# An FFT filter with two dense networks: the opening laid out anew, weight chunks in another order, and the projection's matmuls in runs

## The chip, the cores and the metric

The kernel runs on one core of one Trainium2 chip. The core's engines, with the names that the profile gives them, are TensorE (PE, its weight loads PEld), VectorE (DVE), ScalarE (ACT), GpSimd (POOL) and SyncE (SP), which issues the DMAs. The metric is the device time of one execution in microseconds (us); the time of a kernel is the median of its runs.

## The reference, cut to what matters

Eight batches of 3072 tokens with 256 features pass a filter in the frequency domain along the tokens, then a network with a softmax-weighted hidden layer and a norm, then a network with a gated hidden layer.

```python
X = np.fft.rfft(x, axis=1)                      # x: 8 x 3072 x 256
y = np.fft.irfft(X * (filt_r + 1j * filt_i)[None], n=3072, axis=1)
x = y.reshape(8 * 3072, 256)
h = x @ w_in                                    # 256 -> 1024
e = np.exp(h - h.max(-1, keepdims=True))
solu = h * (e / (e.sum(-1, keepdims=True) + 1e-09))
mu, var = solu.mean(-1, keepdims=True), solu.var(-1, keepdims=True)
x = ((solu - mu) / np.sqrt(var + 1e-06) * g_ln) @ w_out    # 1024 -> 256
h = x @ w_in2                                   # 256 -> 2048
out = (h * (1.0 / (1.0 + np.exp(-1.702 * h)))) @ w_out2    # 2048 -> 256
```

The four weight matrices come as 64-bit floats (the kernel sees words of 64 bits), all else as 32-bit floats.

## The kernel before, in words

**The filter.** A transform of 3072 points is done as 128 x 24. `Filter` takes one or two batches. `load_x` loads a piece of x (128 x 512), `step1` multiplies it by the first transform matrix `dft1`, and `store_a` writes the result to `a_d` in DRAM; a batch has twelve pieces. Then come 32 groups of 96 rows. For each, `load_gt` loads the group's row block (a forward and an inverse matrix of 96 x 96, and the filter's real and imaginary part, 256 columns each), `load_bt` loads its rows of `a_d`, `forward` multiplies by the forward matrix, the product is weighed with the filter, `inverse` multiplies by the inverse matrix, and `store_z` writes z to DRAM. Batch 0 goes alone, as `EarlyFilter`, in plain 32-bit matmuls (each is recorded as two); the others go in pairs, mostly with operands split into a high and a low part (`split`). In `EarlyFilter` POOL copies the halves of the forward matrix in swapped order (`split_m`), a second matmul with this copy (`swap`) gives the rows with real and imaginary part exchanged, and DVE forms the weighed product with three operations (in `forward`, `swap` and `weigh`).

**The weights.** `Weights` cuts the matrices into 24 chunks of 128 x 512 words (512 kB each): four of w1, four of w2, eight of w3, eight of w4, in this order. A chunk is loaded (`load`) into a staging tile (`STAGE`), turned from 64 to 32 bits by DVE operations on its two halves (`magnitude`, `sign`, `lower`, `add`), in w2 and w4 scaled on ACT (`scale_rows`), and split into a high part by ACT (`split_hi`) and a low part by DVE (`split_lo`).

**The networks.** `First(n)` handles block n of 256 tokens, 96 blocks in all: it loads its rows of z, applies the last inverse transform (`y`), multiplies by w1 (`hidden`), computes the softmax weighting and the norm, exchanges blocks through DRAM (`shuffle`, `gather`) and transposes (`turn`), splits (`u_hi`, `u_lo`), and multiplies by w2 (`project`), of which x2s is made. `Second` handles block 0 alone, then pairs of blocks, and the last one alone: 8 or 16 steps of `hidden` with w3, `tanh`, `gate`, two splits and `output` with w4, then `finish` and `store`.

**The order.** No scheduler chooses it. Every step is put into a list with a due time; the list is sorted by due time and the steps are issued in that order, so that on each engine and on SP's queue the program order is the order of due times. One block of `First` has 16 units of due time. The due times of the opening are in `EARLY`: `start1` and `start2` are where batch 0's pieces and groups begin, `end` is where they end, `loads` and `weights` place the chunks. All DMAs are issued by SP, which waits in order: where an issue has to wait for data, all behind it wait too.

```python
end, step1, step2 = v["end"], v["step1"], v["step2"]
start2 = end - v["gap"] - step2 * NG
start1 = start2 - step1 * N2 / 2
```

The projection multiplies, for each half c of its output and each eighth kk of the hidden layer, one w2 high part by 512 columns (high and low part of u) and one w2 low part by 256 columns (the high part of u), all added up in one PSUM tile; two calls per c take four kk each.

Of the kernel before, what the change touches and what calls it, by code (L numbers as in the profile page):

```python
# [83 lines left out]
STAGE = [i % 5 if i < 15 else i % 3 for i in range(24)]  # L84

EARLY = {
    "end": -37.0,
    "step1": 0.73,
    "step2": 0.95,
    "gap": 2.88,  # L90
    "x": (-3.0, 0.1),
    "gt": (-0.01, 1.11),
    "first": (-2.1, 0.0, 0.5),
    "second": (0.3, 0.31, 1.19, 1.3, 2.52, 2.82, 3.47, 4.1, 4.6, 5.3),
    "more": (-2.8, -1.5, 0.0, 0.5),
    "direct": 20,
    "count": 15,
    "between": 4,
    "ahead": ((0.5, 1.45), (1.4, 1.5)),
    "loads": (-81.75, -81.7, -81.86, -77.86, -75.86, -73.86, -71.86, -69.86, -67.86, -65.86, -63.86, -61.86, -59.86, -57.86, -55.86, -46.4, -42.4, -38.4, -34.96, -30.4, -26.12, -22.4, -18.4, -16.17),  # L100
    "weights": ((1.12, 1.9), (-3.5, 4.0)),
    "weight": ((-2.92, -0.81, -0.6, 0.2, 1.29, 1.8, 3.49), (-1.28, -1.05, -0.4, 0.51, 0.79, 1.6, 1.8)),
# [24 lines left out]
def dft_constants():  # L127
# [55 lines left out]
    mats = np.concatenate([fwd2, inv2], 2).transpose(1, 0, 2)  # L183
# [10 lines left out]
def fft_filter_solu_gelu(  # L194
# [48 lines left out]
    dma(out=sgn_sb, in_=sgn)  # L243
# [6 lines left out]
    for b in range(P // Q):  # L250
# [15 lines left out]
    x0 = p1.tile([N1, N2 // 2, 2 * D], F32, tag="w4", name="x0")  # L266
# [4 lines left out]
    class Weights:  # L271
# [28 lines left out]
        def magnitude(self):  # L300
            words = self.raw.rearrange("p k n -> p (k n)").bitcast(I32).rearrange(
                "p (n t) -> p n t", t=2)
            self.low, self.high = words[:, :, 0].bitcast(U32), words[:, :, 1]
            self.mag = p2.tile([P, 512], I32, tag="th", name="w_mag")
# [4 lines left out]
            nc.vector.tensor_scalar(  # L309
                out=self.f, in0=self.f, scalar1=LEAST_HIGH_WORD, scalar2=None, op0=ALU.max)  # L310
            nc.vector.tensor_scalar(
                out=self.mag, in0=self.mag, scalar1=3, scalar2=0x3FFFFFFF,
# [9 lines left out]
        def lower(self):  # L322
            self.wt = p2.tile([P, 512], I32, tag="gl", name="w_wt")
            nc.vector.tensor_scalar(
                out=self.wt, in0=self.top, scalar1=-0x00800000, scalar2=None, op0=ALU.bitwise_and)
            nc.vector.scalar_tensor_tensor(
                out=self.f, in0=self.low, scalar=2.0 ** -52, in1=self.wt.bitcast(F32),
                op0=ALU.mult, op1=ALU.mult)
# [32 lines left out]
    def weight_parts():  # L361
        n = 0
        for dst, src, K, N, gain in (
# [7 lines left out]
            for c in range(0, N, cn):  # L371
                for k in range(0, K, kn):
                    yield Weights(n, dst, src, gain, k, kn, c, cn)
                    n += 1
# [24 lines left out]
    class Filter:  # L399
        pools = {"gt": [(p3, "gt")], "bt": [(p3, "bt")], "az": [(p2, "az")]}  # L400

# [56 lines left out]
        def load_gt(self, g):  # L458
            gt = self.tile("gt", g, [R, 2 * R + 2 * D], F32)
            dma(out=gt, in_=groups[:, g])  # L460
# [3 lines left out]
                m=gt[:, :2 * R],  # L464
# [12 lines left out]
        def forward(self, g):  # L477
# [6 lines left out]
            pr = p2.tile([R, self.nb, D], F32, tag="pr", name="pr")  # L484
# [3 lines left out]
        def swap(self, g):  # L488
            v = self.t[g]
            xw = p2.tile([R, self.nb, D], F32, tag="xw", name="xw")  # L490
            dma(out=xw[:2 * N2], in_=v["xs"][2 * N2:])
            dma(out=xw[2 * N2:], in_=v["xs"][:2 * N2])
            v["xw"] = xw
# [17 lines left out]
        def store_z(self, g):  # L511
            dma(out=self.z_d[:, g].rearrange("b r d -> r b d"), in_=self.t.pop(g)["z"])
# [3 lines left out]
    class EarlyFilter(Filter):  # L516


        pools = {
            "gt": [(p3, "gt")], "bt": [(p3, "bt")] * 3 + [(p2, "xs")] * 2,  # L520
            "az": [(p2, "az"), (p2, "fh"), (p2, "fl")] * 2}
        wide_gt = None

        def tile(self, name, g, shape, dtype):
            if name == "gt" and g % 8 >= 3:

                if self.wide_gt is None:
                    self.wide_gt = p1.tile([shape[0], 5, shape[1]], dtype, tag="u", name="gt")
                return self.wide_gt[:, g % 8 - 3]
            return super().tile(name, g, shape, dtype)  # L530

        def split_m(self, g):
            v = self.t[g]
            v["swap"] = p4.tile([R, R], F32, tag="mt", name="ms")
            nc.gpsimd.tensor_copy(out=v["swap"][:, :R // 2], in_=v["m"][:, R // 2:R])
            nc.gpsimd.tensor_copy(out=v["swap"][:, R // 2:], in_=v["m"][:, :R // 2])
# [4 lines left out]
        def forward(self, g):  # L541
            v = self.t[g]
            f = ps_m.tile([R, self.nb, D], F32, tag="m", name="f2")
            nc.tensor.matmul(f, v["m"][:, :R], v["bt"], start=True, stop=True)
            v["pr"] = p2.tile([R, self.nb, D], F32, tag="pr", name="pr")
            nc.vector.tensor_tensor(v["pr"], f, v["fr"], op=ALU.mult)

        def swap(self, g):
            v = self.t[g]
            f = ps_h2.tile([R, self.nb, D], F32, tag="h2", name="f4")  # L550
            nc.tensor.matmul(f, v["swap"], v["bt"], start=True, stop=True)
            v["xw"] = p2.tile([R, self.nb, D], F32, tag="xw", name="xw")
# [57 lines left out]
    class First:  # L610
# [112 lines left out]
        def project(self, c, f):  # L723
# [250 lines left out]
```

## Time and profile before

| | |
|---|---|
| time, median of 3 runs | 3698.51 us (3698.39 to 3699.56) |
| time of the profiled execution | 3699.28 us |
| its span, first to last instruction | 3697.5 us |
| PE busy | 3600.7 us, 97% of the span, 16768 matmuls |
| DVE busy | 2772.5 us, 75% |
| ACT busy | 2027.7 us, 55% |
| chain of work that ended last | PE 88%, DVE 2%, ACT 1%, issue 1% |

The span is divided in the page into 40 slices of some 92 us; PE's busy tenths there are 6, 7, 7, 9, and 9 in every later slice. Busy times are unions of the instructions' spans. The granted clock of TensorE is given as a share of 2.4 GHz: 1.00 is 2.4 GHz, 0.50 is 1.2 GHz. Shares over a whole span hide that its stages differ, so the rows below are taken by stage.

### The profile page before, as it was taken

How to read it: one execution, taken by the hardware profiler on the slowest of the kernel's cores; microseconds unless marked ns; L12 is line 12 of the kernel's file. 1: busy time of each engine (PE TensorE's matmuls, PEld its weight loads, DVE VectorE, ACT ScalarE, POOL GpSimd, SP SyncE). 2: the span in 40 equal slices, each digit the busy share in tenths (PEclk: the TensorE clock that was granted, in tenths of full speed). 3: DMA queues.
4: the chain of work that ended last, by engine and by line, in shares of the span. 5: the costliest groups of instructions: out<-in, count | busy, mean ns of one | idle time of the engine just before them, and what ended most of it. 6: DMA issues, size and time to landing. Idle time of an engine off the chain costs nothing.

```text
span 3697.5 us, 50701 instructions
## 1 busy us (share of the span) xinstructions
PE 3600.7 (97%) x16768; PEld 2936.2 (79%) x16768; DVE 2772.5 (75%) x4065; ACT 2027.7 (55%) x3762; POOL 869.9 (24%) x1349
## 2 busy tenths in 40 slices
PE   6779999999999999999999999999999999999999
PEld 2357788888888888888888888888888888888887
DVE  7768887667888887767887888667777777676675
ACT  2346665555555555555565656555565555454453
POOL 1123332222222221222222222222222221111110
PEclk6789999999999999999999999999999999999999
DMA  8745554334444443443444444333333432322221
GB/s 255 225 131 150 150 153 122 123 122 115 119 119 119 125 116 103 127 130 109 115 120 123 116 119 117 113 113 106 106 104 106 117 105 74 86 72 79 82 77 30
DMA packets 385671, 433.73 MB, mean 117 GB/s; under 512 B 144128, under 2 KB 294784, under 8 KB 385408
## 3 DMA queue, kind: packets, MB, share of 16 engines
q1 hardware_dynamic: 385408, 430.49, 40.4%
q8 instruction: 132, 2.16, 0.3%
q14 instruction: 131, 1.07, 0.1%
HBM read 232.13 MB, written 176.16 MB: 110 GB/s over the span
## 4 chain that ended last, share of the span: by engine, by line
PE 88%; DVE 2%; ACT 1%; issue 1%; POOL 0%; DMA 0%; POOLq 0%; DVEq 0%; ACTq 0%
PE o L838 27%; PE h L799 27%; PE x L730 14%; PE h L647 13%; PE f L395 5%; PE yt L629 2%; DVE ob L849 0%; DVE gl L823 0%; ACT h L683 0%; DVE xl L638 0%; POOL rs L687 0%; ACT th L806 0%; ACT az L440 0%; ACT u L717 0%; POOL ssq L684 0%
## 5 line engine op out<-in xcount | busy, mean ns | idle before, releaser
L838 PE MATMUL o<-gh,w 128*128 128x512 f32 (+1 forms) x3136 | 962.5, 389 | 2.9 <-DVE ob L849 2.9
L799 PE MATMUL h<-x2s,w_hi 128*128 128x512 f32 (+1 forms) x3136 | 956.5, 387 | 0.2 <-DVE th L811 0.2
L799 PEld LDWEIGHTS h<-x2s,w_hi 128*128 128x128 f32 x3136 | 569.8, 188 | 116.1 <-ACT x2s L748 0.3
L838 PEld LDWEIGHTS o<-gh,w 128*128 128x128 f32 x3136 | 569.5, 188 | 114.2 <-issue 5.0
L823 DVE TENSOR_TENSOR gl<-th,gh 128x512 fp32r<-128x512 f32 x768 | 557.4, 726 | 132.3 <-ACT gh L817 118.2
L817 ACT CAST gh<-th 128x512 fp32r<-128x512 f32 x768 | 471.9, 614 | 336.1 <-DVE th L811 328.4
L838 PE MATMUL o<-gl,w 128*128 128x512 f32 (+1 forms) x1568 | 606.3, 387 | 2.4 <-DVE gl L823 2.3
L806 ACT ACTIVATE th<-h 128x512 f32<-128x512 f32 x768 | 459.2, 598 | 240.1 <-PE h L799 238.6
L730 PE MATMUL x<-u,w_hi 128*128 128x512 f32 x1536 | 557.4, 399 | 8.5 <-DVE u L720 8.5
L811 DVE SCALAR_TENSOR_TENSOR th<-th,h 128x512 f32<-128x512 f32 x768 | 522.2, 680 | 21.4 <-ACT th L806 20.1
L742 DVE TENSOR_TENSOR x_sum<-x,x_sum 128x256 f32<-128x256 f32 x192 | 81.6, 425 | 530.7 <-ACT x_sum L741 530.6
L799 PE MATMUL h<-x2s,w_lo 128*128 128x512 f32 (+1 forms) x1568 | 478.8, 387 | 0.0
L659 ACT ACTIVATE e<-h,nmx 128x1024 f32<-128x1024 f32 x192 | 214.7, 1118 | 415.3 <-DVE nmx L653 373.7
L730 PE MATMUL x<-u,w_lo 128*128 128x256 f32 x1536 | 432.1, 281 | 0.0
L730 PEld LDWEIGHTS x<-u,w_hi 128*128 128x128 f32 x1536 | 290.3, 189 | 81.3 <-DVE u L720 12.6
L663 POOL TENSOR_SCALAR q<-se 128x1 f32<-128x1 f32 x192 | 44.8, 233 | 1316.7 <-ACT e L659 1316.6
L838 PEld LDWEIGHTS o<-gl,w 128*128 128x128 f32 x1568 | 294.5, 188 | 70.2 <-DVE gl L823 9.0
L799 PEld LDWEIGHTS h<-x2s,w_lo 128*128 128x128 f32 x1568 | 292.7, 188 | 63.6
L730 PEld LDWEIGHTS x<-u,w_lo 128*128 128x128 f32 x1536 | 291.6, 190 | 10.9
L741 ACT COPY x_sum<-x 128x256 f32<-128x256 f32 x192 | 71.1, 370 | 394.1 <-PE x L730 394.1
L672 DVE SCALAR_TENSOR_TENSOR e<-h,e 128x1024 f32<-128x1024 f32 x192 | 234.2, 1220 | 19.4
L647 PE MATMUL h<-w_hi,xh 128*128 128x512 f32 x768 | 241.4, 396 | 3.1 <-ACT xh L634 3.1
(84 smaller groups left out, 5266.0 us busy)
## 6 DMA issues: line engine op xcount, KB each, us to landing
e_d<-e SPq DMA_DIRECT2D x192, 512.0 KB, 2.9
e<-e_d SPq DMA_DIRECT2D x768, 128.0 KB, 3.1
gt<-in_groups SPq DMA_DIRECT2D x160, 264.0 KB, 3.7
a_d<-az SPq DMA_DIRECT2D x96, 256.0 KB, 2.6
zr<-z_d SPq DMA_DIRECT2D x96, 256.0 KB, 2.9
out<-ob SPq DMA_DIRECT2D x768, 32.0 KB, 1.6
xin<-in_x SPq DMA_DIRECT2D x84, 256.0 KB, 3.6
bt<-a_d SPq DMA_DIRECT2D x96, 192.0 KB, 3.8
```

The source lines that it names most:

```text
L395: nc.tensor.matmul(out, w[i], x[j], start=m == 0, stop=m == 2)
L647: nc.tensor.matmul(hs, xx[:, c, a * P:(a + 1) * P], ww[:, c, f * 512:(f + 1) * 512], start=(m == 0 and c == 0), stop=(m == 2 and c == 1))
L659: nc.scalar.activation(out=e, in_=self.h[a], func=AF.Exp, bias=self.v[a], accum_out=se)
L672: nc.vector.scalar_tensor_tensor(out=e, in0=self.h[a], scalar=1.0, in1=e, op0=ALU.mult, op1=ALU.mult, accum_out=su)
L730: nc.tensor.matmul(self.x2[c][:, :n].rearrange("p i t -> p (i t)"), w2[i][:, kk, c * P:(c + 1) * P], self.u[:, kk, :n].rearrange("p i a t ...
L742: nc.vector.tensor_tensor(self.xs[:, c], t[:, 0], self.xs[:, c], op=ALU.add)
L799: nc.tensor.matmul(self.part(t, j), ww[:, c, f * P:(f + 1) * P], xx[..., c, :], start=(m == 0 and c == 0), stop=(m == 2 and c == 1))
L806: nc.scalar.activation(out=th, in_=self.t[d], func=AF.Tanh, scale=0.851)
L811: nc.vector.scalar_tensor_tensor(out=self.g[d], in0=self.g[d], scalar=1.0, in1=self.t.pop(d), op0=ALU.add, op1=ALU.mult)
L817: nc.scalar.copy(out=gh, in_=self.g[d])
L823: nc.vector.tensor_tensor(gl, th, gh, op=ALU.subtract)
L838: nc.tensor.matmul(o, ww[:, f, h * P:(h + 1) * P], self.part(gg, j), start=(f == 0 and m == 0), stop=(f == K2 - 1 and m == 2))
```

## The change: what it does

1. **Batch 0.** All twelve loads of x are issued first; the loads of `sgn` and of the gain `g_ln` come later. The host adds to every group's row block a third matrix: the inverse with its two halves of rows exchanged and their signs set (`turned`). `EarlyFilter` loads these for four groups at a time into tiles `mt`. One matmul (`forward`) remains of the two with the forward matrix; DVE multiplies its result at once by the real and the imaginary part (`weigh`, one operation of 512 columns), and `inverse` adds two matmuls in PSUM, one with the inverse and one with the turned inverse. POOL's copies and the swapped matmul go. There are 19 places for the matrices instead of eight (some in the tile that x used), ten places for `bt`, and PE's operands are widened from 96 to 128 rows and columns, with the added rows set to zero by memsets on DVE. `store_a` and `store_z` of batch 0 are issued from ACT's queue instead of SP's.
2. **Weights.** The chunks are taken in the order w1, w2, and then two of w3 and two of w4 in turn (`ORDER`), with staging places in other tiles (`STAGE`) and new due times (`loads`, `convert`). The first DVE operation of a chunk becomes an `Abs` on ACT. Only w1's chunks are converted beside the groups of batch 0.
3. **Order of blocks 0 to 2.** Their due times shift by -2.49, -2.3 and -0.12 units; block 0's second network begins at -0.05 with a spacing of 2.9 units instead of 4.0.
4. **Projection.** For each c, the first call takes all eight wide matmuls, the second all eight narrow ones.
5. In the other batches the tiles `pr` and `xw` become the two halves of one tile `pw`.

The diff, cut to its core:

```diff
-STAGE = [i % 5 if i < 15 else i % 3 for i in range(24)]
+ORDER = [0, 1, 2, 3, 4, 5, 6, 7, 8, 9, 16, 17, 10, 11, 18, 19, 12, 13, 20, 21, 14, 15, 22, 23]
+STAGE = [0, 1, 2, "e", "e", 0, 1, 2, "pw", "pw", 0, 1, 2, "pw", "pw", 0, 1, 2, "pw", "pw", 0, "pw", "pw", "pw"]
 EARLY = {
-    "end": -37.0, "step1": 0.73, "step2": 0.95, "gap": 2.88, "x": (-3.0, 0.1), "gt": (-0.01, 1.11),
+    "end": -36.99, "step1": 25.97, "step2": 0.83, "gap": 6.0, "x": (-8.35, 0.03), "gt": (4.66, 5.2, -4.45),
...
-    "loads": (-81.75, -81.7, -81.86, -77.86, -75.86, -73.86, -71.86, -69.86, -67.86, -65.86, -63.86, -61.86, -59.86, -57.86, -55.86, -46.4, -42.4, -38.4, -34.96, -30.4, -26.12, -22.4, -18.4, -16.17),
-    "weights": ((1.12, 1.9), (-3.5, 4.0)),
+    "opening": (-0.05, 2.9),
+    "shift": (-2.49, -2.3, -0.12),
+    "loads": (-63.46, -85.07, -66.92, -63.78, -40.07, -39.95, -38.89, -39.87, -38.15, -36.42, -35.26, -29.67, -30.46, -26.83, -28.61, -26.9, -23.26, -23.0, -19.51, -21.51, -16.67, -16.56, -10.11, -9.34),
+    "convert": (-61.36, -57.05, -48.5, -52.08, -39.08, -37.53, -36.03, -34.35, -33.55, -30.14, -29.23, -26.36, -27.59, -24.72, -22.78, -21.43, -19.42, -15.97, -16.78, -14.99, -11.07, -11.7, -6.6, -7.06),
+    "weight": (-0.98, -0.23, 0.17, 0.46, 0.65, 1.06, 1.27, 1.37, 1.79, 2.41),
+    "small": (-44.22, -37.8),
...
+    turned = np.roll(inv2, R // 2, axis=1)
+    turned[0] *= sgn[:, :1]
+    turned[1:] *= sgn[:, 1:]
+    mats = np.concatenate([turned, fwd2, inv2], 2).transpose(1, 0, 2)
...
         def magnitude(self):
-            nc.vector.tensor_scalar(
-                out=self.mag, in0=self.high, scalar1=0x7FFFFFFF, scalar2=None, op0=ALU.bitwise_and)
+            nc.scalar.activation(out=self.power, in_=self.high.bitcast(F32), func=AF.Abs)
...
     class EarlyFilter(Filter):
+        send = nc.scalar.dma_start
+
+        def __init__(self, batches):
+            super().__init__(batches)
+            n = 2 * R + 2 * D
+            u = p1.tile([P, 5 * n], F32, tag="u", name="gt")
+            gts = [u[:, i * n:(i + 1) * n] for i in range(5)]
+            gts += [p3.tile([P, n], F32, tag="gt", name="gt") for _ in range(3)]
+            gts += [early[:, i * n:(i + 1) * n] for i in (9, 10, 0, 1, 2, 3, 4, 5, 6, 7, 8)]
...
+            for t in bts + prs:
+                nc.vector.memset(t[R:], 0.0)
+            for t in mts:
+                nc.vector.memset(t[R:], 0.0)
+            for t in gts[:10]:
+                nc.vector.memset(t[R:, :2 * R + P - R], 0.0)
...
+        def load_gt(self, g):
+            gt = self.slot("gt", g)
+            dma(out=gt[:R], in_=groups[:, g, R:])
+            self.t[g] = dict(m=gt, fl=gt[:R, 2 * R:].rearrange("p (t n) -> p t n", t=2))
+            if g % 4 == 0:
+                mt = self.slot("mt", g // 4)
+                dma(out=mt[:R].rearrange("p (g r) -> p g r", g=4), in_=groups[:, g:g + 4, :R])
...
         def forward(self, g):
-            nc.tensor.matmul(f, v["m"][:, :R], v["bt"], start=True, stop=True)
-            nc.vector.tensor_tensor(v["pr"], f, v["fr"], op=ALU.mult)
+            nc.tensor.matmul(v["f"][:, 0], v["m"][:, :P], v["bt"], start=True, stop=True)
         def swap(self, g):
-            nc.tensor.matmul(f, v["swap"], v["bt"], start=True, stop=True)
-            nc.vector.scalar_tensor_tensor(
-                out=v["xw"], in0=f, scalar=sgn_sb[:, min(g, 1):min(g, 1) + 1], in1=v["fi"],
-                op0=ALU.mult, op1=ALU.mult)
+            pass
         def weigh(self, g):
-            nc.vector.tensor_tensor(v["pr"], v["pr"], v["xw"], op=ALU.subtract)
+            nc.vector.tensor_tensor(
+                v["pr"][:R].rearrange("p (t n) -> p t n", t=2),
+                v.pop("f")[:R].to_broadcast([R, 2, D]), v["fl"], op=ALU.mult)
         def inverse(self, g):
-            nc.tensor.matmul(f, v["m"][:, R:], v["pr"], start=True, stop=True)
+            for m, w in enumerate((v["m"][:, R:R + P], v["turned"])):
+                nc.tensor.matmul(
+                    f[:w.shape[1]], w, v["pr"][:, m * D:(m + 1) * D], start=m == 0, stop=m == 1,
+                    skip_group_check=True)
...
         def project(self, c, f):
-            for kk in range(f * K1 // 2, (f + 1) * K1 // 2):
-                for i in range(2):
-                    n = 2 - i
-                    nc.tensor.matmul(
-                        self.x2[c][:, :n].rearrange("p i t -> p (i t)"),
-                        w2[i][:, kk, c * P:(c + 1) * P],
-                        self.u[:, kk, :n].rearrange("p i a t -> p (i a t)"),
-                        start=(kk == 0 and i == 0), stop=(kk == K1 - 1 and i == 1),
+            n = 2 - f
+            for kk in range(K1):
+                nc.tensor.matmul(
+                    self.x2[c][:, :n].rearrange("p i t -> p (i t)"),
+                    w2[f][:, kk, c * P:(c + 1) * P],
+                    self.u[:, kk, :n].rearrange("p i a t -> p (i a t)"),
+                    start=(kk == 0 and f == 0), stop=(kk == K1 - 1 and f == 1),
...
-        plan_second(block, 32.0 * k, 4.0 if k == 0 else 2.0)
+        plan_second(block, *EARLY["opening"] if k == 0 else (32.0 * k, 2.0))
```

## Rows read from the trace of the kernel before

**Rows 1.** Busy time by stage; columns: stretch, engines' busy time, clock, DMA share, GB/s.

```profile
0.00:48.60 48.60, 20.41 (x28) 6.17 (x28) 26.80 (x51) 13.20 (x23) 3.08 (x13) 0.78 0.88 268
48.60:139.50 90.90, 77.13 (x194) 40.78 (x194) 76.84 (x176) 20.94 (x51) 22.26 (x56) 0.65 0.78 219
139.50:218.20 78.70, 51.73 (x141) 28.88 (x142) 51.58 (x84) 35.44 (x69) 13.17 (x19) 0.78 0.70 221
218.20:300.00 81.80, 66.19 (x378) 55.69 (x376) 56.21 (x74) 41.25 (x75) 23.73 (x37) 0.94 0.41 114
300.00:600.00 300.00, 298.44 (x1388) 242.39 (x1387) 259.69 (x369) 195.67 (x365) 94.15 (x127) 1.00 0.54 148
```

**Rows 2.** PE in order of time, groups of batch 0: start, us.

```profile
48.72 1.14 PE L544 MATMUL f<-bt,gt 96*96 96x256 f32 x2 [0.60 <-DMA bt<-a_d]
...
116.47 0.67 PE L544 MATMUL f<-bt,gt 96*96 96x256 f32 x2
...
118.07 0.67 PE L544 MATMUL f<-bt,gt 96*96 96x256 f32 x2
...
123.33 1.14 PE L544 MATMUL f<-bt,gt 96*96 96x256 f32 x2 [3.72 <-DMA bt<-a_d]
...
125.97 1.06 PE L544 MATMUL f<-bt,gt 96*96 96x256 f32 x2
```

**Rows 3.** DVE in order of time: last product of the groups, x2s of block 0.

```profile
139.27 0.42 DVE L560 TENSOR_TENSOR pr<-pr,xw 96x256 f32<-96x256 f32 x1
...
217.49 0.69 DVE L751 TENSOR_TENSOR x2s<-x_sum,x2s 128x512 fp32r<-128x512 f32 x1 [0.69 <-ACT x2s L748]
```

**Rows 4.** Busy time in two stretches of the groups, columns as in rows 1.

```profile
65.20:112.80 47.60, 43.49 (x95) 22.81 (x96) 45.48 (x105) 10.25 (x24) 13.93 (x30) 0.50 0.74 203
112.90:119.60 6.70, 6.49 (x26) 3.59 (x24) 5.56 (x13) 1.75 (x5) 0.99 (x4) 1.00 0.79 215
```

**Rows 5.** SP's queue in order of time: one issue of a store.

```profile
123.03 0.30 SPq L512 DMA_DIRECT2D z_d<-az  x1
```

**Rows 6.** DVE by line, 139.5 to 218.2 us: busy, mean ns, idle before.

```profile
L326 DVE SCALAR_TENSOR_TENSOR w_mag<-wst,w_wt 128x512 f32<-128x512 uint32 x8 | 5.5, 692 | 0.3
L359 DVE TENSOR_TENSOR w<-w_top,w 128x512 fp32r<-128x512 f32 x8 | 5.5, 685 | 0.3 <-ACT w L356 0.3
L331 DVE TENSOR_TENSOR w_mag<-w_mag,w_top 128x512 f32<-128x512 f32 x8 | 5.5, 684 | 0.0
L318 DVE SCALAR_TENSOR_TENSOR w_top<-wst,w_mag 128x512 int32<-128x512 int32 x8 | 5.5, 684 | 0.0
L324 DVE TENSOR_SCALAR w_wt<-w_top 128x512 int32<-128x512 int32 x8 | 4.4, 550 | 0.2
L311 DVE TENSOR_SCALAR w_mag<-w_mag 128x512 int32<-128x512 int32 x7 | 3.9, 564 | 0.2
...
L309 DVE TENSOR_SCALAR w_mag<-w_mag 128x512 f32<-128x512 f32 x7 | 3.0, 427 | 0.2
L307 DVE TENSOR_SCALAR w_mag<-wst 128x512 int32<-128x512 int32 x7 | 3.0, 424 | 12.2 <-DMA wst<-in_w_out 12.2
```

**Rows 7.** DVE by line, 0 to 260 us: a product of 512 columns with PSUM.

```profile
L485 DVE TENSOR_TENSOR pr<-f,gt 96x512 f32<-96x512 f32 x1 | 0.7, 687 | 1.9 <-ACT xs L482 1.9
```

**Rows 8.** PE in order of time: a projection and what follows; the last block.

```profile
1034.42 0.39 PE L730 MATMUL x<-u,w_hi 128*128 128x512 f32 x1
...
1037.23 0.64 PE L799 MATMUL h<-x2s,w_hi 128*128 128x512 f32 x2
...
3662.41 0.62 PE L838 MATMUL o<-gh,w 128*128 128x512 f32 x2
...
3663.77 0.40 PE L799 MATMUL h<-x2s,w_hi 128*128 128x256 f32 x2
...
3665.21 0.63 PE L838 MATMUL o<-gh,w 128*128 128x512 f32 x2
```

**Rows 9.** DMA issues, 0 to 300 us: count, KB each, us to landing.

```profile
wst<-in_w_in SPq DMA_DIRECT2D x12, 512.0 KB, 5.6
```

More of the change, by code (lines that the diff above doesn't have):

```diff
@@ L82 @@
 }
-STAGE = [i % 5 if i < 15 else i % 3 for i in range(24)]
+ORDER = [0, 1, 2, 3, 4, 5, 6, 7, 8, 9, 16, 17, 10, 11, 18, 19, 12, 13, 20, 21, 14, 15, 22, 23]
+STAGE = [0, 1, 2, "e", "e", 0, 1, 2, "pw", "pw", 0, 1, 2, "pw", "pw", 0, 1, 2, "pw", "pw", 0, "pw", "pw", "pw"]
 EARLY = {
[L87 to L95, printed above, removed]
-    "direct": 20,
-    "count": 15,
-    "between": 4,
-    "ahead": ((0.5, 1.45), (1.4, 1.5)),
-    "loads": (-81.75, -81.7, -81.86, -77.86, -75.86, -73.86, -71.86, -69.86, -67.86, -65.86, -63.86, -61.86, -59.86, -57.86, -55.86, -46.4, -42.4, -38.4, -34.96, -30.4, -26.12, -22.4, -18.4, -16.17),
-    "weights": ((1.12, 1.9), (-3.5, 4.0)),
-    "weight": ((-2.92, -0.81, -0.6, 0.2, 1.29, 1.8, 3.49), (-1.28, -1.05, -0.4, 0.51, 0.79, 1.6, 1.8)),
+    "end": -36.99,
+    "step1": 25.97,
+    "step2": 0.83,
+    "gap": 6.0,
+    "x": (-8.35, 0.03),
+    "gt": (4.66, 5.2, -4.45),
+    "first": (-1.3, -0.46, 5.21),
+    "second": (-0.4, 0.64, 1.73, 1.99, 2.68, 3.25, 3.99, 4.34, 4.91),
+    "more": (-2.73, -1.19, 0.91, 1.34),
+    "direct": 20,
+    "between": 0,
+    "ahead": ((-20.99, -0.21), (1.01, 1.32)),
+    "opening": (-0.05, 2.9),
[4 more added lines that the diff above has]
+    "small": (-44.22, -37.8),
 }
@@ L248, in blocks, with load_gain @@
         return slice(b * Q, (b + 1) * Q), rows[b * K1 * Q:(b + 1) * K1 * Q]
-    for b in range(P // Q):
+    def load_gain(b):
         part, rows = blocks(g_ln, b)
@@ L287, in load @@
         def load(self):
-            if self.n < EARLY["count"] and self.n % 5 > 2:
-                self.raw = p2.tile(self.shape, U64, tag="e", name="wst")
+            if STAGE[self.n] in ("e", "pw"):
+                self.raw = p2.tile(self.shape, U64, tag=STAGE[self.n], name="wst")
             else:
@@ L372, in weight_parts @@
                 for k in range(0, K, kn):
[L373 removed]
+                    yield Weights(ORDER.index(n), dst, src, gain, k, kn, c, cn)
                     n += 1
@@ L489, in swap @@
             v = self.t[g]
[L490 to L493, printed above, removed]
+            dma(out=v["xw"][:2 * N2], in_=v["xs"][2 * N2:])
+            dma(out=v["xw"][2 * N2:], in_=v["xs"][:2 * N2])
         def weigh(self, g):
@@ L532, in split_m, with load_bt @@
+        def load_bt(self, g):
+            assert self.stored == self.steps
+            bt = self.slot("bt", g)
+            dma(out=bt[:R], in_=self.a_d[0, g])
+            self.t[g]["bt"] = bt
         def split_m(self, g):
[L533 to L536, printed above, removed]
+            pass
@@ L892, in fft_filter_solu_gelu @@
             start1 + step1 * i + d for d in v["first"]],
-        lambda g: [start2 + step2 * g + d for d in v["second"][1:]],
+        lambda g: [start2 + step2 * g + d for d in v["second"]],
         lambda g: (
-            start1 + v["gt"][0] + v["gt"][1] * g if g < 8
-            else start2 + step2 * g + v["second"][0]))
+            start1 + v["gt"][0] + v["gt"][1] * g if g < 10
+            else start2 + step2 * g + v["gt"][2]))
+    for b in range(P // Q):
+        at(v["small"][0], load_gain, b)
+    at(v["small"][1], lambda: dma(out=sgn_sb, in_=sgn))
     def dense(g):
@@ L919, in fft_filter_solu_gelu @@
         plan_filter(batches, lambda i: [piece(i - 4) + d for d in FILTER["first"]], second)
[L920 to L923 removed]
+    for w in weight_parts():
+        i = w.n
+        t = v["convert"][i]
         steps = (
[L925 to L926 removed]
+            w.magnitude, w.clamp, w.shift, w.sign, w.exponent, w.lower, w.add, w.scale_rows,
+            w.split_hi, w.split_lo)
+        in_order(v["loads"][i], t + v["weight"][0])
         at(v["loads"][i], w.load)
[L928 to L929 removed]
+        in_order(*v["weight"])
+        for d, step in zip(v["weight"], steps, strict=True):
             at(t + d, step)
```

83 lines of the change are left out of this document (42 added, 41 removed).

## The prediction

> **What bounds the kernel now.** I read the busy time by stage first, then the order of TensorE (PE) and VectorE (DVE) within the stages, then single operations. In [rows 1] the reader is to compare PE's busy time and clock with the length of each stage. From 300 us on PE is busy 298.4 of 300 us at full clock: the rest of the kernel is a row of matmuls without gaps, and only a shorter row would shorten it. Before 300 us it is otherwise: PE is busy 20.4 of 48.6, 77.1 of 90.9 (at a mean clock of 0.65), 51.7 of 78.7 and 66.2 of 81.8 us. So the end moves with the opening as far as later work, already gap-free, starts earlier.
>
> The opening has four parts. Batch 0 is loaded and transformed until the first matmul over a group at 48.72 us [rows 2]. The 32 groups follow, until DVE's last product at 139.27 us [rows 3]. Then block 0 is brought to the second network, with x2s ready at 217.49 + 0.69 = 218.2 us [rows 3]; I count to the start, 217.5. Last the pipeline fills until 300 us. In the second part DVE is the limit: 45.5 of 47.6 us busy between 65.2 and 112.8 us [rows 4], since it converts ten weight chunks beside the groups.
>
> **The first part of the opening.** The change loads dft1 and all of x before anything else, and ten sets of group matrices behind them; five small loads go away from the front, and three weight chunks that went between the pieces of x wait. Bytes until the last a_d store: x 3.15 MB, a_d 3.15, dft1 0.13, ten matrix sets at 270 kB, three turned sets at 147 kB, one chunk of 0.52: 10.1 MB. At the 268 GB/s of this stage in [rows 1] that is 37.7 us, but not all of it must be through. I take 36 us for the first group matmul; 28 if the stores overtake the matrices, 44 if they are all in front.
>
> Storing a_d and z from ACT's queue takes 44 issues there, at 0.30 us like SP's [rows 5], 13 us in all; I cost them at nothing, for ACT is busy only 20.9 of 90.9 us in the group stage [rows 1]. With that cover gone it is 13 us. SP in turn no longer waits for those copies with loads queued behind it. The 28 memsets on DVE have at most 512 columns; at the 0.43 us of such an operation [rows 6] they take 12 us, under loads that last 36, because no chunk is converted then.
>
> **The groups.** Three matmuls of 256 columns per group before and after; the third now multiplies by the host's swapped inverse, and PSUM adds. DVE's three operations become one of 512 columns, near 0.69 us [rows 7], and GpSimd's two copies go. Only four chunks are converted here instead of ten. DVE then needs 32 x 0.69 + 4 x 4.3 = 39 us and is no limit. Two others remain. PE: a group took 118.07 - 116.47 = 1.60 us at full clock and 125.97 - 123.33 = 2.64 at half [rows 2], so 51 us or 84. DMA: what is left after 10.1 MB (22 matrix sets, five turned sets, a_d and z at 3.15 MB each, three chunks) is 14.5 MB, 54 us at 268 GB/s. The trace held half clock (1.2 GHz) from 65.2 to 112.8 us although PE was busy 43.5 of 47.6 us, and full clock (2.4 GHz) from 112.9 to 119.6 us with 6.5 of 6.7 busy [rows 4]. In the new stage PE no longer waits for DVE and its tiles are padded from 96 to 128 rows and columns, so I take full clock and 55 us, ends 48 and 84. The last DVE product comes at 36 + 55 = 91 us instead of 139.3, 48 earlier.
>
> The turned matrices arrive in pieces of 384 bytes, which no row here prices; I leave them at the rate above. The Trainium skill (DMA: Bandwidth & Descriptors, Specifications) asks for at least 512 bytes and names a read-modify-write below that; were it to double these 1.18 MB, the sum would be 4 us higher, an estimate.
>
> **From the groups to x2s.** Here the bill comes back. In [rows 6] eight chunks are converted in this stage; after the change it is twenty, since only the four of w1 come earlier, and by its due times the last chunk (-4.65 and -4.19) still stands about at x2_lo of block 0 (-4.86) in DVE's order. So neither the order in pairs nor the other staging places bring the second network forward here; I cost both at nothing. One chunk loses its first DVE operation, 0.42 us, to ACT (Abs); the seven others sum to 0.692 + 0.685 + 0.684 + 0.684 + 0.550 + 0.564 + 0.427 = 4.29 us. Twenty are 86 us. The rest of DVE in the stage is 51.6 [rows 1] less the chunks' 37.0 (36.3 in [rows 6] and one more subtraction of 0.7), 14.6. Together 100 us if DVE never idles; with their starts overlapping and the operations at their shortest 88, with one tenth idle 112. The stage took 217.5 - 139.3 = 78.2 us and now takes 100: 22 back. x2s of block 0 starts at 191 us instead of 217.5, 26.5 earlier, with the same matmuls done by then.
>
> **Filling the pipeline.** Block 0's second network runs at 2.9 instead of 4 units, so more of it stands early, where PE had 81.8 - 66.2 = 15.6 us idle [rows 1]. Blocks 1 and 2 still need their own chain. I take 5 us, between 0 and 12. The shifted blocks 0 to 2 are in these terms; the one tile for pr and xw changes no wait, as forward already waited for pr.
>
> **The projection in runs.** It takes 192 sequences of eight wide and eight narrow matmuls. Alternating, one took 1037.23 - 1034.42 = 2.81 us [rows 8]. In runs, six wide ones took 3663.77 - 3662.41 = 1.36 us, 227 ns each, and twelve narrow ones 3665.21 - 3663.77 = 1.44, 120 ns each [rows 8]. Eight and eight are 2.776 us: 0.034 less, 6.6 us over 192. I take 7; 0 and 9 are the ends. Nothing waits longer, since the first matmul needs all of u either way.
>
> The Trainium skill (TensorE: Matmul & The Clock Gate, Back-to-back issue gap) gives N/2.4 + 2.5 ns at full clock, 216 and 109 ns, whatever stands before. By that the order is worth nothing and the sum is 7 us higher. The trace has 227 and 120 ns in runs and 351 for a pair, so I go by the rows.
>
> **Sum.** 26.5 + 5 + 7 = 38.5 us off the profiled execution's 3699.3: 3660.8. That execution lies 0.8 us above the median of the three runs, so 3660 us, 1.0% faster.
>
> **Rivals.** First, the clock stays at half in the groups: 84 instead of 55 us, 3660 + 29 = 3689. For it speaks the long half-clock stretch at 91% busy [rows 4]; against it that PE would then be the limit, without gaps, and the trace has full clock where PE was busy 6.5 of 6.7 us.
>
> Second, on the other side: the chunks come too late. Abs stands first on ACT, in order, so a late chunk now stops ACT and with it the copies, exp and squares that PE and DVE need, where it stopped DVE alone. Already DVE waited 12.2 us for seven chunks here [rows 6], 1.7 each, and a chunk of 512 kB takes 5.6 us from issue to landing [rows 9]; now twenty come in 100 us, on an SP queue that also waits for block data. At 1.7 us each it costs 35 us: 3695, no change. From 38.5 + 7.4 = 46 us, 2.3 per chunk, it is slower by over 0.2%; at 3 us each 3720. Against it speaks that DVE, the busier engine, has other work to fill such waits; and by due times most chunks are issued two to three units before their Abs, where a unit of this stage is 100 us / 35.7 = 2.8 us, so 6 to 8 us.
>
> Third, DVE packs better and the fill gains more: 88 us and 12 us, 3660 - 12 - 7 = 3641. For it speaks 96% busy in [rows 4].
>
> Fourth, the order of the projection is worth nothing, because the extra 4 ns per pair come from what surrounds it: 3667.
>
> **Chances.** 0.2% of 3698.5 is 7.4 us, about what a measurement of this kernel tells from no change. Forecast 0.42; half clock 0.12; late chunks 0.16, of it 0.09 within 0.2% and 0.07 slower; better packing 0.18; projection without gain 0.12. Faster by over 0.2%: 0.42 + 0.12 + 0.18 + 0.12 = 0.84; within: 0.09; slower: 0.07. The range reaches from 5 us under the better packing to the half clock and the edge of no change: 3636 to 3691. It leaves out the late chunks and a little below.
>
> **What the new profile would show.** First group matmul near 36 us; the groups 1.7 us apart at granted clock 1.0; the last DVE product of the groups near 91; DVE busy over 90% from there to x2s near 191; PE gap-free from about 260; a projection of sixteen in 2.78 us. It would be wrong if ACT shows long waits for in_w loads, if the groups run at 0.5, or if PE's gaps after 191 us are larger than before.

## The result, and the profile after

The changed kernel takes 3664.4 us (median of 4 runs, 3660.6 to 3665.8) against 3699.0 (3698.4 to 3699.6) for the kernel before: a ratio of 0.9905, 95% interval 0.9888 to 0.9922. The forecast was 3660, its range 3636 to 3691. The profiled execution took 3660.6 us, with a span of 3658.7: 38.8 us less than the span of before. It lies 3.8 us under the median of its runs; the medians of the two kernels differ by 34.6 us.

Busy time by stage, columns as in [rows 1]; the stages end at the first group matmul, the last DVE product of the groups, x2s of block 0, and two later points.

```profile
0.00:34.40 34.40, 13.91 (x24) 4.47 (x24) 8.87 (x29) 8.61 (x14) 0.29 (x5) 0.82 0.97 312
34.40:87.50 53.10, 44.85 (x181) 34.09 (x182) 35.30 (x59) 15.10 (x37) 0.00 (x0) 0.96 0.92 261
87.50:191.20 103.70, 62.91 (x161) 33.55 (x160) 92.37 (x159) 57.83 (x110) 16.52 (x19) 0.72 0.83 257
191.20:273.70 82.50, 70.43 (x380) 60.13 (x380) 59.54 (x80) 44.81 (x81) 24.91 (x37) 0.88 0.43 125
273.70:573.70 300.00, 298.36 (x1390) 242.74 (x1389) 258.12 (x367) 195.25 (x365) 93.03 (x127) 1.00 0.53 145
```

PE in order of time in the groups, which answers to [rows 2]:

```profile
34.44 3.19 PE L586 MATMUL f<-bt,gt 128*128 128x256 f32 x6 [13.79 <-DMA bt<-a_d]
...
40.42 0.59 PE L586 MATMUL f<-bt,gt 128*128 128x256 f32 x2
...
41.71 0.59 PE L586 MATMUL f<-bt,gt 128*128 128x256 f32 x2
...
56.47 0.67 PE L586 MATMUL f<-bt,early 128*128 128x256 f32 x2 [0.41 <-DMA bt<-a_d]
```

DVE in order of time, which answers to [rows 3]:

```profile
87.53 0.69 DVE L594 TENSOR_TENSOR pr<-f,early 96x512 f32<-96x512 f32 x1 [0.61 <-PE f L586]
...
191.24 0.68 DVE L789 TENSOR_TENSOR x2s<-x_sum,x2s 128x512 fp32r<-128x512 f32 x1
```

The first group matmul comes at 34.4 us (before 48.7), the last product at 87.5 (139.3), x2s of block 0 at 191.2 (217.5). So 26.3 of the 38.8 us are there when block 0 reaches the second network. A group without waits takes 41.71 - 40.42 = 1.29 us. What shortened the groups (fewer chunks beside them, one operation on DVE instead of three, full clock) was not tried apart, but for the run with four more chunks beside them, below. The bill for the postponed conversions is the third stage: 103.7 us where it was 78.2.

DVE and ACT by line from 87.5 to 191.2 us, columns as in [rows 6]: the dearest conversion, the first DVE operation of a chunk, and Abs on ACT ahead of it.

```profile
L338 DVE SCALAR_TENSOR_TENSOR w_mag<-wst,w_wt 128x512 f32<-128x512 uint32 x20 | 14.8, 742 | 0.3
...
L316 DVE TENSOR_SCALAR w_wt<-w_wt 128x512 f32<-128x512 f32 x20 | 8.4, 422 | 6.0 <-ACT w_wt L313 6.0
```

```profile
L313 ACT ACTIVATE w_wt<-wst 128x512 f32<-128x512 f32 x20 | 13.3, 668 | 16.4 <-DMA wst<-in_w_out 7.7 <-DMA wst<-in_w_in 5.8 <-DVE w_mag L338 2.9
```

Twenty chunks it is, as forecast. But DVE is busy 92.4 of 103.7 us, and 6.0 of its 11.3 idle us wait for Abs, which itself waits 13.5 us for loads.

What DMA moved up to x2s of block 0, first of the changed kernel (0 to 191.2 us), then of the kernel before (0 to 217.5):

```profile
DMA packets 33161, 51.24 MB, mean 268 GB/s; under 512 B 7936, under 2 KB 15744, under 8 KB 33152
```

```profile
DMA packets 30108, 50.34 MB, mean 231 GB/s; under 512 B 4752, under 2 KB 12560, under 8 KB 30096
```

The bytes are nearly the same. The opening is shorter with its transfers packed denser.

### The profile page after: what moved, and what is told of

Read it like the earlier page. It is cut to its first block, busy times and chain, and to the rows that moved or that the text cites. A ratio compares the mean times of both kernels' runs of the same rounds, so it can differ in the third digit from the quotient of the medians.

```text
span 3658.7 us, 50562 instructions
## 1 busy us (share of the span) xinstructions
PE 3564.5 (97%) x16768; PEld 2936.7 (80%) x16768; DVE 2751.7 (75%) x4005; ACT 2041.4 (56%) x3786; POOL 849.1 (23%) x1285
## 4 chain that ended last, share of the span: by engine, by line
PE 89%; DVE 3%; DMA 3%; ACT 2%; issue 1%; POOL 0%; SPq 0%; POOLq 0%; DVEq 0%; ACTq 0%
PE o L878 27%; PE h L839 27%; PE x L768 15%; PE h L686 13%; PE f L407 5%; PE yt L668 2%; DMA a_d<-az 1%; DVE gl L863 1%; DVE ob L889 0%; DMA zr<-z_d 0%; ACT h L722 0%; DMA wst<-in_w_in 0%; ACT th L846 0%; DVE nmx L692 0%; PE f L449 0%
## 5 line engine op out<-in xcount | busy, mean ns | idle before, releaser
L839 PEld LDWEIGHTS h<-x2s,w_hi 128*128 128x128 f32 x3136 | 577.5, 189 | 113.7 <-ACT x2s L786 0.4
L768 PE MATMUL x<-u,w_hi 128*128 128x512 f32 x1536 | 384.5, 393 | 7.3 <-DVE u L759 6.1
L878 PEld LDWEIGHTS o<-gl,w 128*128 128x128 f32 x1568 | 294.6, 188 | 70.7 <-DVE gl L863 11.4
L748 DVE STREAM_TRANSPOSE ut<-e 128x1024 f32<-128x1024 f32 x192 | 237.0, 1234 | 6.5 <-DMA e<-e_d 6.4
L686 PE MATMUL h<-w_hi,xl 128*128 128x512 f32 x768 | 238.3, 392 | 0.1
```

The source lines that it names most:

```text
L686: nc.tensor.matmul(hs, xx[:, c, a * P:(a + 1) * P], ww[:, c, f * 512:(f + 1) * 512], start=(m == 0 and c == 0), stop=(m == 2 and c == 1))
L748: nc.vector.transpose(out=self.ut[a].rearrange("p k (i t) -> p k i t", t=Q), in_=self.e.pop(a).rearrange("p (i k f) -> p k i f", i=P // Q, ...
L768: nc.tensor.matmul(self.x2[c][:, :n].rearrange("p i t -> p (i t)"), w2[f][:, kk, c * P:(c + 1) * P], self.u[:, kk, :n].rearrange("p i a t ...
L839: nc.tensor.matmul(self.part(t, j), ww[:, c, f * P:(f + 1) * P], xx[..., c, :], start=(m == 0 and c == 0), stop=(m == 2 and c == 1))
L878: nc.tensor.matmul(o, ww[:, f, h * P:(h + 1) * P], self.part(gg, j), start=(f == 0 and m == 0), stop=(f == K2 - 1 and m == 2))
```

## The experiments

The table gives for each profiled execution the first group matmul, the last DVE product, x2s of block 0 and of block 10, the end of the span, and the time from x2s of block 10 to that end, all in us. The last column splits the opening from the rest.

| kernel | first | last product | x2s 0 | x2s 10 | end | x2s 10 to end |
|---|---|---|---|---|---|---|
| before | 48.7 | 139.3 | 217.5 | 603.1 | 3697.5 | 3094.4 |
| changed | 34.4 | 87.5 | 191.2 | 575.1 | 3658.7 | 3083.6 |
| changed, again | 34.3 | 89.6 | 195.4 | 579.7 | 3662.6 | 3082.9 |
| runs alone | 47.7 | 137.7 | 214.8 | 603.0 | 3686.4 | 3083.4 |
| alternating | 35.3 | 90.1 | 196.2 | 579.5 | 3674.4 | 3094.9 |
| 96 rows | 33.8 | 87.4 | 191.3 | 574.6 | 3658.2 | 3083.6 |
| stores on SP | 36.9 | 92.8 | 202.1 | 587.0 | 3671.0 | 3084.0 |
| Abs on DVE | 34.3 | 90.5 | 197.9 | 581.9 | 3665.1 | 3083.2 |
| w2 beside groups | 34.7 | 105.2 | 201.6 | 585.9 | 3669.1 | 3083.2 |
| no low words | 33.1 | 86.3 | 185.7 | 570.1 | 3653.5 | 3083.4 |
| half chunks | 33.7 | 85.1 | 184.9 | 568.3 | 3651.8 | 3083.5 |
| half, no low | 33.9 | 84.9 | 174.9 | 558.7 | 3641.9 | 3083.2 |
| spacing 4 | 34.9 | 89.4 | 193.3 | 579.3 | 3663.0 | 3083.7 |
| four places for x | 35.4 | 92.3 | 193.7 | 576.2 | 3660.3 | 3084.1 |

The changed kernel, run again as it is, was expected thus:

> The changed kernel itself, as a control beside the others of this call: 3660 to 3666, x2s of block 0 between 188 and 197 us, since the changed kernels so far differed by 5 us in the opening.

It took 3664.1 us (3658.3 to 3664.8). All eight runs of the two sets lie between 3658.3 and 3665.8, and the two profiles differ by 4.1 us at x2s of block 0 and by 3.9 at the end: executions differ in the opening. A difference of 3 us between two versions is therefore none. It matters, too, which execution was profiled: the one of the changed kernel lies 3.8 us under its median, the second one 0.5 over.

**The projection in runs, alone.** The kernel before, with this edit and nothing else:

```diff
-            for kk in range(f * K1 // 2, (f + 1) * K1 // 2):
-                for i in range(2):
...
+            n = 2 - f
+            for kk in range(K1):
...
```

> The kernel before with the projection in runs and nothing else of the change. If the order of wide and narrow matmuls is what pays (prediction: 7 us; the spacing of x2s from block to block in the new profile says up to 11): 3688 to 3692, and a projection of sixteen takes 2.78 us. If the order is worth nothing, as the page's formula has it, and the blocks come closer together for another reason of the change: 3698 to 3700.

3689.1 us (3686.7 to 3690.7) against 3700.0 for the kernel before in the same set, ratio 0.9969 (0.9959 to 0.9980): 10.9 us faster. DVE's x2s of blocks 10 and 95, in order of time, of the kernel before and of this one:

```profile
603.05 0.69 DVE L751 TENSOR_TENSOR x2s<-x_sum,x2s 128x512 fp32r<-128x512 f32 x1
...
3643.32 0.69 DVE L751 TENSOR_TENSOR x2s<-x_sum,x2s 128x512 fp32r<-128x512 f32 x1
```

```profile
602.96 0.69 DVE L750 TENSOR_TENSOR x2s<-x_sum,x2s 128x512 fp32r<-128x512 f32 x1
...
3632.25 0.68 DVE L750 TENSOR_TENSOR x2s<-x_sum,x2s 128x512 fp32r<-128x512 f32 x1
```

At block 10 both stand at 603.0; 85 blocks later this one is 11.1 us ahead. The rival, that the order is worth nothing, falls.

**Everything but the runs.** The changed kernel with the projection alternating as before (the edit above, reversed):

> The changed kernel with the projection alternating as before. If the two parts of the change add up: 3671 to 3676, with x2s of block 0 still near 191 us. If the order is worth nothing: 3662 to 3666. If the runs pay only together with the new opening, e1 and e2 do not add up to 35 us.

3676.6 us (3674.3 to 3678.8), ratio 0.9938 (0.9921 to 0.9955): 12.2 us slower than the changed kernel. In the table the last column tells the runs from the alternating order without exception: 3082.9 to 3084.1 against 3094.4 and 3094.9, some 11.2 us over 86 blocks. PE in order of time shows where. First two half projections of the changed kernel, each with the other matmuls behind it, then the same of the alternating one:

```profile
999.78 1.98 PE L768 MATMUL x<-u,w_hi 128*128 128x512 f32 x8
1001.60 0.61 PE L839 MATMUL h<-x2s,w_hi 128*128 128x512 f32 x2
...
1002.96 1.11 PE L768 MATMUL x<-u,w_lo 128*128 128x256 f32 x8
1003.91 0.63 PE L878 MATMUL o<-gh,w 128*128 128x512 f32 x2
...
1005.29 1.98 PE L768 MATMUL x<-u,w_hi 128*128 128x512 f32 x8
```

```profile
1041.96 0.39 PE L769 MATMUL x<-u,w_hi 128*128 128x512 f32 x1
...
1043.36 0.63 PE L840 MATMUL h<-x2s,w_hi 128*128 128x512 f32 x2
...
1044.75 0.39 PE L769 MATMUL x<-u,w_hi 128*128 128x512 f32 x1
...
1046.15 0.63 PE L879 MATMUL o<-gh,w 128*128 128x512 f32 x2
...
1047.54 0.39 PE L769 MATMUL x<-u,w_hi 128*128 128x512 f32 x1
```

In runs the sixteen take 1.82 + 0.95 = 2.77 us, alternating 1.40 + 1.40 = 2.80 (2.81 in one piece, [rows 8]). But the six 512-column matmuls behind each half differ too: 1.36 us behind wide ones and 1.38 behind narrow ones, against 1.39 and 1.39. All in all 5.51 us against 5.58, 0.07 for each half c of the output; over the 172 of 86 blocks that is 12 us, where 11.2 were measured.

**Groups on 96 rows.** The groups' matmuls without the padding to 128:

```diff
-            nc.tensor.matmul(v["f"][:, 0], v["m"][:, :P], v["bt"], start=True, stop=True)
+            nc.tensor.matmul(v["f"][:R, 0], v["m"][:R, :R], v["bt"][:R], start=True, stop=True)
```

and the two matmuls of `inverse` likewise.

> The changed kernel with the matmuls of the groups on 96 rows and 96 columns again, all else as it is. If the widening to 128 is what keeps the clock up: the granted clock of the groups falls towards 0.5, a group takes 2.6 us instead of 1.6 where PE sets the pace, the last product comes at 100 to 117 instead of 88 us, and the whole takes 3672 to 3693. If what kept the clock low before was PE's waiting for VectorE: clock above 0.9 in the groups, 3661 to 3667.

3661.5 us (3660.0 to 3666.3), the groups through at 87.4 us, with a granted clock of 0.97 from 39.0 to 87.4 us. The padding changes nothing, so it isn't what held the clock in the groups.

**The stores back on SP.** a_d and z of batch 0 are stored from SP's queue again:

```diff
-        send = nc.scalar.dma_start
```

> The changed kernel with the stores of a_d and z of batch 0 on SP's queue again. If the stores block the loads behind them: the first product comes 5 to 10 us later, the groups also take longer, 3668 to 3680. If the queue does not matter, because the same DMA engines move the same bytes, as I costed it: 3661 to 3667.

3669.1 us (3666.8 to 3672.8), ratio 0.9918 (0.9903 to 0.9933): 5 us slower than the changed kernel, with no run inside its eight. The chain of waits of SP's queue, 0 to 92.8 us (queue and line, what it waits for, total us, times, longest), names the copies that it waits for:

```profile
SPq L524 <- ACT z L608: 9.8, 9, 3.9
SPq L458 <- ACT az L453: 5.2, 4, 1.9
```

The first group matmul comes at 36.9 us and the last product at 92.8, the first later than in any other run with the new opening, the second than in any but the one with w2 beside the groups. The profiled execution lies 3.7 us over its median.

**Abs on DVE.** The chunk's first operation goes back to DVE, at the place of the clamp, so that a late chunk no longer stops ACT:

```diff
-            nc.scalar.activation(out=self.power, in_=self.high.bitcast(F32), func=AF.Abs)
+            nc.vector.tensor_scalar(
+                out=self.wt, in0=self.high, scalar1=0x7FFFFFFF, scalar2=None, op0=ALU.bitwise_and)
```

> The changed kernel with the first operation of a weight chunk on VectorE again, at the place of the second. If VectorE sets the time from the last product of the groups to x2s, twenty operations of 0.42 us come on it: 8 us more there, x2s near 199 us, 3670 to 3674. If instead the waits of ACT for late chunks set it (the Abs stops ACT in order), taking the Abs off ACT makes it the same or up to 8 us faster: 3656 to 3664.

3669.5 us (3667.2 to 3674.1), ratio 0.9920 (0.9905 to 0.9935): 5 us slower. The stage behind the groups, columns as in [rows 1]:

```profile
91.20:197.90 106.70, 61.89 (x157) 32.80 (x155) 100.16 (x179) 47.37 (x91) 17.20 (x19) 0.71 0.81 248
```

DVE's work rises from 92.4 to 100.2 us, but the stage only from 103.7 (105.8 in the second profile) to 106.7: most of the added work fell into time in which DVE had waited for Abs. So the load of DVE alone doesn't set this stage.

**w2 beside the groups.** The four chunks of w2 are loaded and converted beside the groups, where DVE has time:

```diff
-    "loads": (..., -40.07, -39.95, -38.89, -39.87, ...
+    "loads": (..., -59.5, -55.5, -51.0, -46.9, ...
-    "convert": (..., -39.08, -37.53, -36.03, -34.35, ...
+    "convert": (..., -54.5, -50.3, -45.5, -42.5, ...
```

The load of the small vectors moves ahead of them.

> The changed kernel with the four chunks of w2 loaded and converted beside the groups of batch 0, where VectorE is busy 34.6 of 51.2 us, instead of after them. If VectorE sets the stretch from the groups to x2s, that stretch loses 4 x 4.1 = 16 us, the groups gain what four chunks cost the DMA there (4 x 1.9 = 8 us at most), and the whole is 3 to 12 us faster: 3652 to 3661. If what counts in the groups is also VectorE, or the stretch is a chain of waits, nothing is won: 3662 to 3672.

3673.1 us (3670.9 to 3674.4), 9 us slower than the changed kernel: a miss. Busy time from the first group matmul on, and from the groups' end to x2s:

```profile
35.20:105.90 70.70, 51.28 (x188) 38.45 (x186) 49.61 (x87) 22.54 (x53) 0.00 (x0) 0.88 0.83 228
105.90:201.60 95.70, 58.87 (x153) 31.25 (x153) 78.42 (x132) 50.20 (x96) 14.31 (x19) 0.75 0.81 253
```

DVE by line in the groups (43 to 105 us):

```profile
L316 DVE TENSOR_SCALAR w_wt<-w_wt 128x512 f32<-128x512 f32 x8 | 3.4, 425 | 13.1 <-ACT w_wt L313 13.1
```

The later stage does shrink, by some 7 us (201.6 - 105.2 = 96.4), but the groups end 17.7 us later. DVE stands still 13.1 us for eight chunks, 1.6 each, and the groups' products are queued behind. This is the mechanism of the second rival, at the price that I gave it there (1.7 us per chunk). But it is only a part of the 17.7 us: the changed kernel has 6.0 us of this wait for its four chunks there, so 7.1 came on top, and the bytes of the groups rose from 13.87 to 16.1 MB, some 9 us at 261 GB/s by my estimate. No run separates the two.

**No low words.** DVE's operations `exponent` and `lower` are left out, and the addition only copies the high word, so the weights lose their low words; 20 chunks need 21 us less of DVE.

```diff
-            nc.vector.tensor_scalar(out=self.wt, in0=self.top, ...)
-            nc.vector.scalar_tensor_tensor(out=self.f, in0=self.low, ...)
-            nc.vector.tensor_tensor(self.f, self.f, self.top.bitcast(F32), op=ALU.add)
+            nc.vector.tensor_tensor(self.f, self.top.bitcast(F32), self.top.bitcast(F32), op=ALU.max)
```

> The changed kernel without the two VectorE operations that make and scale a weight's low word (1.11 us of some 4.3 per chunk), so that the low words are left out of the weights; the addition becomes a copy of the high word. If VectorE's load sets the stretch from the groups to x2s: 20 x 1.1 = 22 us less there, x2s at 168 to 174 us, 3641 to 3648. If late chunks and the DMA rate set it (257 GB/s in that stretch): less than 10 us off, 3654 to 3662.

3661.2 us (3655.4 to 3663.4), 3 us below the changed kernel. The stage, and DVE's first operation in it (86 to 185 us):

```profile
87.00:185.70 98.70, 57.96 (x157) 31.34 (x155) 71.65 (x118) 57.43 (x111) 13.57 (x19) 0.76 0.86 268
```

```profile
L316 DVE TENSOR_SCALAR w_wt<-w_wt 128x512 f32<-128x512 f32 x20 | 8.5, 424 | 16.3 <-ACT w_wt L313 16.3
```

With 20.7 us less to do, DVE ends the stage 5 us sooner; its wait for Abs grows from 6.0 to 16.3 us. That DVE's load sets the stage falls here.

**Half of every chunk's bytes.** Only the first half of a raw chunk is loaded, and read twice:

```diff
-                dma(out=self.raw[part], in_=src)
+                if kn == 1:
+                    dma(out=self.raw[part][:, :, :cn // 2], in_=src[:, :, :cn // 2])
+                else:
+                    dma(out=self.raw[part][:, :kn // 2], in_=src[:, :kn // 2])
...
```

> The changed kernel, with only the first half of every raw weight chunk loaded; the other half of each converted chunk is made from the same bytes again, so the weights are wrong in one half and every engine does the same work. 24 x 0.26 = 6.3 MB are left out of the 51.24 MB that the changed kernel moves up to x2s of block 0. Theory A, the transfers set the end of the opening: at the same 268 GB/s 44.95 MB take 168 us, but DVE's 92 to 93 us of work behind the groups then stands as the next limit, so x2s of block 0 at 172 to 181 us instead of 191 to 195, and 3642 to 3654 us against 3664. Theory B, DVE's load or the order of the plan sets it and the transfers run beside: x2s at 187 to 195, 3658 to 3667 us.

**And both at once**, half of the bytes and no low words (the last two edits together):

> Both at once: half of every raw chunk left out as in the run before, and DVE's two operations per chunk for the exponent and the low words left out too, so the weights lose their low words. Leaving out the two operations alone gave 3661.2 us, with x2s of block 0 at 185.7 in a stage whose DVE was 72 of 99 us busy. Theory A, transfers and DVE are two limits close to each other, and taking away one alone shows little: both together give x2s at 155 to 170 us and 3622 to 3644 us, more than the sum of the two alone. Theory B, the order of the plan or a wait that is neither bytes nor DVE sets the end: no more than the two alone, x2s at 180 to 187, 3650 to 3662 us.

3653.5 us (3653.0 to 3657.3) and 3648.7 us (3643.8 to 3649.6). The stage in the first and in the second:

```profile
85.80:184.90 99.10, 59.89 (x157) 31.11 (x155) 92.00 (x159) 57.38 (x111) 16.01 (x19) 0.76 0.71 215
```

```profile
85.60:174.90 89.30, 57.24 (x157) 30.53 (x155) 70.68 (x119) 57.52 (x111) 13.36 (x19) 0.77 0.76 235
```

By the medians leaving out the low words was worth 3 us, half of the bytes 11, and both 16. At x2s of block 0 the profiles have 5.5, 6.3 and 16.3, with the 4 us by which executions differ; the second of these is of an execution at its median, the other two, like the changed kernel's, of executions 4 to 6 us under theirs. So both count, the loads more by the medians: but 20.7 us of DVE's work bring 3 to 6, and 6.3 MB, 24 us at the stage's 257 GB/s (20 of them in the stage itself, which has twenty of the 24 chunks), bring 6 to 11. Theory A has the time of the first run, at the edge of its range, and not that of the second; 3648.7 lies between its 3644 and the 3650 of theory B. Neither theory has x2s in either run. The two together bring about the sum of the two alone, and not more, as they would if each had hidden the other. With the bytes halved DVE is busy 92.0 of 99.1 us; with both gone it is busy 70.7 of 89.3, with DMA at 0.76, and something third is left.

**Four places for the pieces of x.** One candidate for it was SP, which waits for PE to free a piece of the next batches:

```diff
-                xt = p2.tile([N1, 2 * D], F32, tag="xin", name="xin")
+                xt = p2.tile([N1, 2 * D], F32, tag="fl" if i0 % 2 and i0 < self.direct else "xin", name="xin")
```

> The changed kernel with four places instead of two for the pieces of x of the next two batches that come beside the weight chunks (every odd piece lies in a tile that is idle then); every engine's order and all bytes are the same. Behind the groups the trace of the changed kernel has SP waiting 25.4 us in 15 times, up to 3.6 us, for PE to free such a piece, with chunk loads queued behind it. Theory A, this ring is the third limit, which kept the runs with half of the bytes and without low words from gaining more: SP's waits go, x2s of block 0 at 180 to 188 us instead of 191 to 195, and 3650 to 3659 us against 3664. Theory B, bytes and DVE are the limits, and the ring only spreads the same transfers: x2s at 189 to 196, 3660 to 3667 us.

3661.9 us (3661.5 to 3662.2), x2s at 193.7: not told apart from the changed kernel. SP's waits behind the groups, of the changed kernel and of this one:

```profile
SPq L439 <- PE f L449: 25.4, 15, 3.6
```

```profile
SPq L458 <- ACT az L453: 26.4, 15, 3.7
```

The wait is as long as before and stands one instruction later, at the store of the same piece: SP, in order, now waits for ACT's copy. The ring of places isn't the third limit, and theory A falls. But SP's waits did not go, as theory A had supposed they would, so whether they are a limit stays open. Nor did any run touch another wait on the same pieces: with half of the bytes and no low words (85 to 175 us) ACT stands still before its copies of them until an older piece's store to `a_d` has landed, 10.2 us in 8 times.

```profile
ACT az L460 <- DMA a_d<-az: 10.2, 8, 2.4
```

**The second network of block 0 in steps of 4.**

```diff
-    "opening": (-0.05, 2.9),
+    "opening": (0.0, 4.0),
```

> The changed kernel with the second network of block 0 planned as before, in steps of 4 units with no offset, and nothing else different. My forecast gave the filling of the pipeline 5 us: 3667 to 3671 us against 3664 of the changed kernel. The profile after found some 1 us there: 3662 to 3667. Rival, the tighter steps cost DVE and ACT more than they bring: 3655 to 3661.

3670.7 us (3664.9 to 3674.0). By the median 6 us slower, as my forecast had it; but the profiled execution, 5.7 us under the median, shows 386.1 us from x2s of block 0 to that of block 10, only 2.2 more than the changed kernel's 383.9. The edit is worth 2 to 6 us; these runs scatter too much to say more.

That the chunks alternate in pairs (`ORDER`) was not tried apart from the rest.

## Why the prediction came right, point by point

**First group matmul: 36 forecast, 34.4 measured.** Right, and the 10.73 MB of that stage lie near my 10.1; they came at 312 GB/s, where I had taken 268.

**Groups: 55 forecast, 53.1 measured.** Right. The clock is full from 39.1 to 93.7 us, so the half-clock rival falls. My row for PE's period (1.60 us) was too long: a group without waits takes 1.29 us, 41 us for 32, and I put the rest down to DMA, at 0.92 and 13.87 MB; my 54 us for the transfers was the better term. That padding helps to hold the clock was a reason of mine, and it falls. What did hold it isn't shown.

**ACT's stores: costed at nothing.** What the 44 issues cost ACT no run shows by itself. That SP is rid of them and of the waits for the copies I named without a price; with the cost on ACT taken off, it is worth 5 us by the medians. With the stores on SP the profile has 36.9 and 55.9 us, so my 36 and 55 fit the kernel without this part as well as with it: there I was lucky.

**Groups to x2s: 100 forecast, 103.7 measured (105.8 in the second profile).** The size was right, the cause only in part. I had DVE never idle: 86 us for chunks and 14.6 of other work. It was busy 92.4 us and idle 11.3. So I had 8 us too much work and left 11 us of waiting out, and that the two nearly cancel is luck. Taking 20.7 us of its work away brought 3 us in the median, halving the chunks' bytes 11, and adding 7.8 us of work lengthened the stage by 1 to 3. The stage is a row of chunks, each passing from its load through ACT's Abs to DVE and back to ACT, in fixed order on every queue, and none of the three runs shows one engine that bounds it. What the third share is, with loads and DVE both relieved, stays open.

**The rival of late chunks** is there, but smaller: ACT waits 13.5 us for loads in the stage, 0.7 per chunk where the rival had 1.7, and DVE has other work for half of it. Put beside the groups, chunks do cost 1.6 us each.

**Filling: 5 forecast.** From x2s of block 0 to that of block 10 it is 385.6 us before and 383.9 after; if 1.3 of this belongs to the projection (10 blocks by 0.13), the fill gave 0.4 us, and 1.7 at most. This is the step that failed. With the spacing of 4 units the same stretch takes 386.1 us, so by these profiles, one of each kernel, the tighter spacing brings 2.2 us, and something else in the change takes part of it back. What that is stays open. It isn't the earlier x2s of block 0 as such: in the other eleven profiles with the new opening it lies anywhere from 174.9 to 202.1 us, and the stretch takes 382.5 to 384.9.

**Projection: 7 forecast, 11 measured.** Mechanism right, size too small: I priced the sixteen matmuls alone, and the wide matmuls that follow them gain as much. The Trainium skill (TensorE: Matmul & The Clock Gate, Back-to-back issue gap) gives an isolated matmul's gap by its own width alone, and by that there is no gain; two pairs of kernels, 10.9 and 12.2 us apart, speak against it for matmuls of unlike width.

**The sum.** 26.3 at x2s, 1.7 to block 10 and 10.8 behind it are the 38.8 us of the profile, against 26.5 + 5 + 7 = 38.5 forecast: the fill was too large and the projection too small by about the same. But that execution lies 3.8 us under its median. The second profile, near the median, has 22.1, 1.3 and 11.5, together 34.9, and the medians differ by 34.6: there the opening brings 4 us less than forecast. The mechanism is in the main the one forecast; that the sum fits so closely is in part luck.

No version here beats the changed kernel by more than its own executions differ, among those that compute all of it.

## What to carry to other kernels

Before calling a stage bound by an engine at 90%, count its idle time and what ends it: here 20.7 us of its work could go for a gain of 3 by the medians, 24 us of transfers for 11, and both for 16, about the sum. Price a change in the order of matmuls with those that follow, not only with the ones reordered. A store that waits for its producer on an in-order queue holds up the loads behind it: moving 44 of them to the producer's own queue gave 5 us, for their issue and their waits together.

## What the runs showed of the hardware

Mixing matmuls of 512 and 256 columns costs a little: two half projections with the matmuls behind them took 5.58 us alternating and 5.51 in runs, and six 512-column matmuls 1.38 or 1.39 us behind 256-column ones and 1.36 behind 512-column ones. Over 86 blocks the order makes some 11.2 us, and each of the fourteen profiles lies on the side where its order puts it. Nearly the same bytes (50.34 and 51.24 MB) went through at 231 and at 268 GB/s up to x2s of block 0, in the kernel before and in the changed one. And the opening differs between two profiled executions of one program by 4.1 us at x2s of block 0, while the 3083 us behind block 10 repeat within 1.2 in twelve profiles.
